# Masks of attention scores on 64-row halves, two groups of scores joined, one sum for the tokens' bound, and a new order, on one core of a Trainium2 chip

## The chip, the cores and the metric

The program runs on one core of a Trainium2 chip. The time is the device time of one execution in microseconds (us); several executions are timed and their median is given. The core has a matrix engine (PE), whose weight loads are shown apart (PEld), a vector engine (DVE), a scalar engine (ACT), GpSimd (POOL), and a queue engine (SP) that issues the transfers between the chip's main memory and the on-chip buffers.

## The reference, cut to what matters

Block-causal attention, whose result goes through two feed-forward layers. All arrays are 32-bit floats.

```python
B, H, S, D = 4, 8, 576, 64             # batch, heads, positions, head size
scores = q @ k.T / sqrt(D)             # a query of block i sees keys of blocks 0..i, blocks of 64
scores = where(block_i >= block_j, scores, -1e9)
attn = softmax(scores); x = attn @ v   # 2304 tokens of 512
h = x @ w_in;  x = (h * tanh(softplus(h))) @ w_out      # layer 0: 512 -> 2048 -> 512
h = relu(x @ w2_in);  out = (h * h) @ w2_out            # layer 1
```

## The kernel before

**Work and stages.** The 2304 tokens are cut into six chunks of 384 (`NX`). Chunks 0 and 1 hold the first 192 positions of the four sequences (`attention_lo`, products in 32-bit floats). Chunks 2 to 5 hold the other 384 positions of one sequence each (`attention_hi`, four pairs of heads in a chunk, 16 pairs in all). Each chunk then makes one pass through layer 0 and one through layer 1 (`PASSES`, twelve passes). Numbers there are split into two 16-bit halves, and each product is three 16-bit products (high by high, low by high, high by low). The last five passes of layer 0 and 1 that are listed in `SEVEN` use a scheme with fewer products (`first_seven`, `second_seven`).

**Scores.** `attention_hi` makes the scores of a pair of heads for three tiles of 128 queries (2, 3 and 4). The first head's 64 rows of queries and keys lie on partitions 0 to 63, the second's on 64 to 127, so a product of one head uses 64 rows of the array and the two heads' products go to two banks. `scores` issues six products (three for each head) and, where the tile reaches the end of what a query may see, two masks: a product of `above` (ones in the columns of the first 64 queries) with `never` (-1e24), which adds a huge negative number to the last 64 keys of those queries. The masks use all 128 rows. Tile 2 has 320 keys; beside it in the same banks the last 128 keys of tile 4 are scored; then tile 3 with 448 keys, then the first 448 keys of tile 4 without a mask. Each group is read by DVE (`peak`, the maximum, L919) and by ACT (`expo`, the exponential, L930), and the pair of banks, `ab`, is free for the next group only after that.

**The tokens' bound.** `chunk_scale` makes the scales of a chunk. Its `norm` bounds the length of a token: ACT squares two halves of the chunk (L1295, L1298), DVE adds them (L1301, L1302), PE sums over the partitions with a product of 384 columns (L1303), and DVE takes the maximum over the 384 tokens (L1305). It runs for 11 of the 12 chunk passes, five times in layer 0.

**Order.** Every piece of work is a task with an engine, some with a choice of engines. `PLAN` holds the whole order, one place and one engine for each task, and was worked out ahead by the planner in `Sched`, whose costs stand in the `sch.add` calls. Each engine takes its instructions in that order, and waits by semaphores for what they need. SP issues transfers in order too.

**Weights.** The split weights of the layers lie in main memory (`wspill`) and are loaded again in each pass, 512 KB at a time, into a ring of buffers (L1244); a load can start when PE has read the last of what the buffer held.

Of the kernel before, what the change touches and what calls it, by code (L numbers as in the profile page):

```python
# [68 lines left out]
def seg_len(tiles):  # L69
# [34 lines left out]
    "8=N{<R|WoF$|;}830D24i}Yj87=)Hj5tj)vNV0U79>g=xv+7ZqCI693uI$k_S@SP>L$>KQeN}qPK~~)-2XvUcDC@DfhxC*`^#k7bk=u#M5bXb3-;vEa4Xu01"
    "NO@cC;N744x;!Db$!qc#?^o(A@|g^i2W6{vm6iH`+EHq;>i^_-ZH0bA<VjhFmb>*0xmE_t*LYaKR#~oN2{!z$FG*urqF2du{PLjGmj(K*&e0k&Pshr$_)_&p"
    "{X(nDZ2e51kSg-2PSj8EcMF-OQ}I$O=`6eSeVwAeV$oP){iRk$?|1OVXSxC3=joI3u};%Zk@~vaqFv-sDT%h@!Rw1?nZmA#p!7PqpVQw$`rR^GM-!J)X08qZ"
    "x6S0Vj@4W7OA*sV8b}v;lNh}KGG9c)k$QvtM{5!Z=lL{kCwKBbPp>hp+50>ZY$@I31b)lbCh|1iI3k0HLq|D9lsd>Uy$9Uym9Bb9d+S|tjT~nGer&u=x1jIs"
    "AZ@qYqc>@3b5J|WGkANAY$39%$k*%f<yl>)KB#zH+RE?JLVuNCWsf%1zOqc)>3q3f+v;5Tl~a~zFYw=7C&^vXOt03p<m0E(hurTj^>sGcl1C)#;FX?IS1ZV9"
    "ayMHS@Tj5l!Cyu5zPvA$^uM6R*T-anbdWjvqKuOvvRq5)`|>X6nnF~*A*N&GTOwau-XxlHiQFie3;L?zjW=bQOyJ%)ouG$xq>L~h=nJySzADe7`8(kEDw!ys"
    ">(}}TxEW%;CUyh)>|y-^Ff>>u>T_UrARc}gWWI^)enfW+SH94<%m^a*g!CmRAD35noZ{Tq^dadb56cjwKM&4tmVc4$PsvUlr}u!C?b^`{lzv3vS=pqI>Wz4K"  # L110
    "ki5W(!SaZ_uMcS(tnMrQr6UNs0W9y<f9oThaxEBsLLSy7+JM(BWL{_OubWugRC?=A)Q|hMH+eN18F%Tww4Th+fqIADNuKng{#3*Jcasa(OTyeq)#(d{W)b%r"
    "sEpm@A$)W_UhE<d=vSb9iryr*lbtt7FK~Z@Ow#T$N*ii-Z7Vg2*Kq8qDz&MSRpnZwci?JUZBN#10ST9bk*l>iC@U%Lh|>japjV4~w3K@6YbGPfp@%@~mHMjI"
    "MB4@+zBc)G9}z7<#x$bp4k33NlC2G;kW|orv@-V!fWtb{pNxHyJ=LgZH-WFm$dU*35%l<*h(1UhTWJCxPY|`G$mfOR%mrH!nGN{+0ZdT^nHOzkUPns>B6?EK"
    "*>dDrS>jQU+FMG7Qnx*F?=W>dTld?dRI;J+v>ddnV4xE6x7};c!Yj{E@A}JQBCylrl0agANd+(cWTf%%`3T~we6~7*8kR@AcEBbtP@{Vz=REK31&!zJJ>>sj"
    "nPz)}z7u53VCu^WJI!o_Resl__7*hx(mo>($QtmFPL3X-rgr4rVQ`kF*W&X-I)fN&1T*PWt)F$hZN;t@WX~Mkr;ViuS+Pe~*xlq_CotKC+*xAllHYsq^$O6m"
    "Jg9?h@p)@-SXCBjYa-K;O57Ek^`vH8CzEwGC%5HlI~b}herY46jH{K4z{eC==L)#6Df@(oPlIviP^l(Th3b-z4MEqn;Hf<*`cAKrqDYvmL(%_o`AR<kCkgVd"
    "5qg)Sel*5o<zUe-^ku!A2#o`GuYt>I@-E0J%K0aBGu-`>ZX{Y2k#R&vP#>?L+SHTP#CAV;c@g$2DNCgb$as<6HDr-IO9iV!rQAgAtSG+Bm&@eIfLqhZ{qk`5"
    "K@e32H0Gky9<ZN6Zk*Q1@N`|Q@aZu&YjrvWpE|P0)`Eo`lh>0!kY9_M`X1Wl+U2?`?@jcoNOpDL>`czP4m=t#mkML1;L~H&)|Zjze3^!Ks}jkTREQP2Q>ROo"
    "ETxk<3g%1W*N3UGpXPydQ1Cf>HtAOF2RogIX~u(%he7aGF#NETkrq_0KFGWe3BAd}KahSe{ZT5<d7xyO?&aR^RFkftL5Ow^Y?c8#&gZmE@IyB_WwNOZ`?Rw;"
# [1768 lines left out]
```

## Time and profile before

| what | us |
|---|---|
| median of 3 runs | 872.76 (871.6 to 872.84) |
| the profiled execution | 872.93 |
| its span, first to last instruction | 871.2 |
| PE busy | 854.1 |
| DVE busy | 765.2 |
| ACT busy | 620.7 |
| POOL busy | 71.7 |

The profiled execution took 1.7 us more than its span, the time around the first and last instruction. Starts of matmuls are measured; their ends are modelled and overlap the next ones, so the cost of a matmul is read from one start to the next, not from its duration.

### The profile page before, as it was taken

How to read it: one execution, taken by the hardware profiler on the slowest of the kernel's cores; microseconds unless marked ns; L12 is line 12 of the kernel's file. 1: busy time of each engine (PE TensorE's matmuls, PEld its weight loads, DVE VectorE, ACT ScalarE, POOL GpSimd, SP SyncE). 2: the span in 40 equal slices, each digit the busy share in tenths (PEclk: the TensorE clock that was granted, in tenths of full speed). 3: DMA queues.
4: the chain of work that ended last, by engine and by line, in shares of the span. 5: the costliest groups of instructions: out<-in, count | busy, mean ns of one | idle time of the engine just before them, and what ended most of it. 6: DMA issues, size and time to landing. Idle time of an engine off the chain costs nothing.

```text
span 871.2 us, 19004 instructions
## 1 busy us (share of the span) xinstructions
PE 854.1 (98%) x7233; PEld 605.1 (69%) x7233; DVE 765.2 (88%) x1830; ACT 620.7 (71%) x1220; POOL 71.7 (8%) x78
## 2 busy tenths in 40 slices
PE   7999999999999999999999999999999999999997
PEld 6665455555555555555777677777878787799997
DVE  6999999999999998899999999996677777779876
ACT  6999999988898786887798987783334253266332
POOL 0000100112211000001000110001000001120100
PEclk9999999999999999999999999999999999999999
DMA  9995699998898998699999999996676746775572
GB/s 343 372 344 208 214 211 225 258 332 281 304 297 179 253 178 274 207 267 273 277 270 316 302 239 259 249 271 206 206 266 252 241 147 231 265 279 164 170 257 90
DMA packets 163930, 217.23 MB, mean 249 GB/s; under 512 B 107520, under 2 KB 125952, under 8 KB 163840
## 3 DMA queue, kind: packets, MB, share of 16 engines
q1 hardware_dynamic: 163840, 216.04, 82.9%
q8 instruction: 56, 0.92, 0.4%
q14 instruction: 34, 0.28, 0.1%
HBM read 160.95 MB, written 29.88 MB: 219 GB/s over the span
## 4 chain that ended last, share of the span: by engine, by line
PE 74%; DVE 10%; ACT 8%; DMA 5%; issue 2%; POOLq 0%; DVEq 0%; SPq 0%; ACTq 0%
PE acc L1453 27%; PE hp L1374 20%; PE hp L1341 12%; PE acc L1492 4%; DMA arena<-wspill 3%; PE bank L908 3%; PE bank L1016 2%; PE acc L1419 2%; DMA qk<-in_qk_dram 1%; ACT wsq L1160 1%; PE bank L1492 1%; ACT pad L930 1%; PE hp L1405 1%; DVE pb L817 1%; DMA arena<-in_w_dram 1%
## 5 line engine op out<-in xcount | busy, mean ns | idle before, releaser
L1453 PE MATMUL acc<-g,arena 128*128 128x384 f16 x1560 | 299.9, 326 | 1.2 <-DMA arena<-wspill 1.0
L1453 PEld LDWEIGHTS <-arena 128*128 128x128 f16 x1560 | 146.6, 98 | 82.6 <-issue 2.6
L1374 PEld LDWEIGHTS <-arena 128*128 128x128 f16 x1194 | 100.8, 98 | 14.4 <-DMA arena<-wspill 1.1
L1341 PE MATMUL hp<-xt,first 128*128 128x384 f16 x528 | 101.3, 326 | 0.8 <-ACT h L1346 0.7
L817 DVE SCALAR_TENSOR_TENSOR g<-h,cst,g 128x768 f16<-128x768 f32 x72 | 73.5, 1020 | 5.1 <-ACT g L1119 3.2
L1341 PEld LDWEIGHTS <-first 128*128 128x128 f16 x528 | 49.5, 98 | 40.4 <-issue 9.8
L1341 PE MATMUL hp<-xt,arena 128*128 128x384 f16 x384 | 75.1, 326 | 1.1 <-DMA arena<-wspill 0.9
L1374 PEld LDWEIGHTS <-first 128*128 128x128 f16 x816 | 69.2, 98 | 7.2 <-issue 0.3
L817 DVE SCALAR_TENSOR_TENSOR pb<-pad,st,pb 128x512 f16<-128x512 f32 (+2 forms) x96 | 71.5, 748 | 3.0 <-ACT pb L950 2.6
L930 ACT ACTIVATE pad<-bank,st,sq 128x448 f32<-128x448 f32 (+1 forms) x96 | 65.1, 681 | 8.8 <-DVE st L924 4.5
L1374 PE MATMUL hp<-arena 128*128 128x192 f16 x660 | 65.9, 246 | 0.0
L950 ACT ACTIVATE pb<-pad,st 128x384 f16<-128x384 f32 (+2 forms) x83 | 58.0, 713 | 4.9 <-DVE st L942 1.8
L919 DVE TENSOR_REDUCE st<-bank 128x1 f32<-128x448 f32 (+1 forms) x96 | 52.3, 572 | 6.9 <-PE bank L911 4.3
L1374 PE MATMUL hp<-xt,arena 128*128 128x192 f16 x534 | 54.4, 246 | 0.4 <-DMA arena<-wspill 0.4
L1346 ACT ACTIVATE h<-hp,cst 128x384 f32<-128x384 f32 x76 | 42.7, 575 | 16.6 <-PE hp L1341 15.9
L1341 PEld LDWEIGHTS <-arena 128*128 128x128 f16 x384 | 36.1, 98 | 26.0 <-DMA arena<-wspill 2.2
L1120 POOL TENSOR_SCALAR g<-h,cst 128x768 f16<-128x768 f32 x23 | 23.5, 1020 | 339.2 <-ACT h L1395 139.1
L1395 ACT ACTIVATE h<-h,cst 128x576 f32<-128x576 f32 x40 | 30.8, 771 | 28.8 <-DVE h L1393 28.7
L1391 ACT ACTIVATE h<-hp,cst 128x192 f32<-128x192 f32 x40 | 16.7, 418 | 47.5 <-PE hp L1374 40.8
L1374 PE MATMUL hp<-arena,first 128*128 128x192 f16 x480 | 50.2, 246 | 0.0
L1208 DVE TENSOR_TENSOR arena<-arena 128x256 f32<-128x256 f32 x96 | 41.5, 433 | 0.9
L1119 ACT ACTIVATE g<-h,cst 128x768 f16<-128x768 f32 x40 | 37.1, 928 | 6.2 <-PE acc L1453 2.9
(327 smaller groups left out, 1746.8 us busy)
## 6 DMA issues: line engine op xcount, KB each, us to landing
arena<-wspill SPq DMA_DIRECT2D x93, 512.0 KB, 4.7
arena<-in_w_dram SPq DMA_DIRECT2D x27, 1023.8 KB, 7.0
arena<-uspill SPq DMA_DIRECT2D x44, 512.0 KB, 5.6
wspill<-arena SPq DMA_DIRECT2D x24, 512.0 KB, 4.2
arena<-wspill SPq DMA_DIRECT2D x32, 384.0 KB, 4.2
qk<-in_qp_dram SPq DMA_DIRECT2D x16, 480.0 KB, 5.2
uspill<-xt SPq DMA_DIRECT2D x12, 512.0 KB, 5.0
uspill<-arena SPq DMA_DIRECT2D x12, 512.0 KB, 5.4
```

The source lines that it names most:

```text
L817: return sch.add("DVE", c_dve(n) + 62 * ap, lambda: nc.vector.scalar_tensor_tensor(dst(), a(), s() if ap else s, c(), op0, op1), r=r, w=w, ...
L919: t = sch.add("DVE", c_dve(o1 - o0), lambda hd=hd: nc.vector.reduce_max(st.t[:, 2 * j + hd:2 * j + hd + 1], pp.t[hd][:, o0:o1], axis=AX.X) ...
L930: t = sch.add("ACT", c_act(o1 - o0, True, 3), lambda hd=hd: nc.scalar.activation(pf[hd].t[r0:, k0:k0 + o1 - o0], view(hd)[r0:, o0:o1], AF. ...
L950: "ACT": ("ACT", c_act(n, False, 1), lambda pb=pb, pv=pv, s=s: nc.scalar.activation(pb.t[:, 0:i + 1, 0, :], pv(), AF.Copy, scale=s()), False),
L1119: "ACT": ("ACT", c_act(n, False, 1), lambda: nc.scalar.activation(dst(0), src(), AF.Copy, scale=s()), False),
L1208: plus(ENG["ts"], 256, lambda e, o=o, x=x, y=y, op=op: e.tensor_tensor(b(o), b(x), b(y), op), [], [q])
L1341: nc.tensor.matmul(out=hp.t[:, 0:n], lhsT=w.t[:, f % 2, a, 128 * k:128 * k + 128], rhs=x.t[:, c, k, 0:n], start=k == 0 and i == 0, stop=k ...
L1346: sch.add("ACT", c_act(n, True, 1), lambda f=f, o=o, hp=hp: nc.scalar.activation(h.t[:, o * n:o * n + n], hp.t[:, 0:n], (AF.Mish, AF.Relu) ...
L1374: nc.tensor.matmul(out=bank.t[:, o:o + z], lhsT=lhs, rhs=x.t[:, c, ks[k], :], start=start and k == 0 and i == 0, stop=k == 1 and i == 2, s ...
L1395: sch.add("ACT", c_act(3 * z, False, 1), lambda: nc.scalar.activation(h.t[:, z:2 * n], h.t[:, z:2 * n], fn, scale=hs()), r=[(cst, (HS, j)) ...
L1453: nc.tensor.matmul(out=acc.t[:, 0:n], lhsT=wo.t[:, f % 2, a, 128 * m:128 * m + 128], rhs=g.t[:, c, f % 2 * n:f % 2 * n + n], start=f == 0 ...
L1492: nc.tensor.matmul(out=acc[bank].t[:, o:o + c1 - c0], lhsT=lhs, rhs=g.t[:, c, z * b + c0:z * b + c1], start=j == 0 and (bank, o) in first ...
```

## The change

- The masks of `attention_hi` are cut in two: the first head's uses rows 0 to 63 of `above` and `never`, the second's rows 64 to 127. Each now sums 64 rows, not 128.
- The scores of tile 2 and of the last 128 keys of tile 4 become one task, so nothing stands between them on PE.
- In layer 0, `norm` no longer makes the maximum over tokens of their squared lengths: ACT sums the squares over all 384 tokens of a partition while it squares (`accum_out`), PE sums over the partitions with a product of 2 columns, DVE adds the two. The bound is then the sum over the chunk. Layer 1 keeps the old form (6 times).
- `never`, `signs` and the new sums `nf` lie in one small tile.
- Planning costs of one-column products (30 for 120 to 163), of the scores and of the products with the values are changed, and `PLAN` is another order.

```diff
+    small = cp.tile([128, 8], F32, name="small")
+    never, signs = small[:, 0:1].bitcast(BF16), small[:, 2:4]
+    R["nf"] = fixed([small[:, 4:6], small[:, 6:8]])
...
-        step = sch.add("PE", 150.0, lambda: nc.tensor.matmul(
+        step = sch.add("PE", 30.0, lambda: nc.tensor.matmul(
             out=vm.t[:, 0:1], lhsT=ones, rhs=upper(sv.t[:, 4:5]), start=True, stop=True), r=[(sv, 4)], w=[vm])
...
-        def scores(i, pp, o, k0, k1, mask=True):
-
-            a = tile_q(i)[0] - q0
+        def scores(pp, *spans):
 
             def mm():
-                for p, (u, w) in enumerate(((0, 0), (1, 0), (0, 1))):
-                    for hd in range(2):
+                for i, o, k0, k1, mask in spans:
+                    a = tile_q(i)[0] - q0
+                    for p, (u, w) in enumerate(((0, 0), (1, 0), (0, 1))):
+                        for hd in range(2):
+                            rows = slice(64 * hd, 64 * hd + 64)
+                            nc.tensor.matmul(out=pp.t[hd][:, o:o + k1 - k0], lhsT=qh.t[rows, u, a:a + 128], rhs=qh.t[rows, w, nq + k0:nq + k1],
+                                             start=p == 0, stop=p == 2 and not mask)
+                    for hd in range(2 if mask else 0):
                         rows = slice(64 * hd, 64 * hd + 64)
-                        nc.tensor.matmul(out=pp.t[hd][:, o:o + k1 - k0], lhsT=qh.t[rows, u, a:a + 128], rhs=qh.t[rows, w, nq + k0:nq + k1],
-                                         start=p == 0, stop=p == 2 and not mask)
-                for hd in range(2 if mask else 0):
-                    nc.tensor.matmul(out=pp.t[hd][:, o + k1 - k0 - 64:o + k1 - k0], lhsT=above, rhs=never[:, 0:1].to_broadcast([128, 64]), start=False, stop=True)
-
-            steps.append(sch.add("PE", 3 * (c_mm16(k1 - k0) + 16) + (110.0 if mask else 0.0), mm, r=[(qh, (p, j)) for p in range(2) for j in range(2)], w=[(pp, 0), (pp, 1)]))
+                        nc.tensor.matmul(out=pp.t[hd][:, o + k1 - k0 - 64:o + k1 - k0], lhsT=above[rows], rhs=never[rows, 0:1].to_broadcast([64, 64]), start=False, stop=True)
...
-            scores(i, pp, 0, 0, n)
+            scores(pp, (i, 0, 0, n, True), *([(4, n, 448, 576, True)] if i == 2 else []))
             if i == 2:
                 last, tail = R["st"].new(), R["tl"].new()
-                scores(4, pp, n, 448, 576)
                 steps.append(halves(vs, v3, sv, R["vm"].new()))
...
+            if l == 0:
+                nf, sq = R["nf"].new(), R["nsq"].new()
+                for i, k in enumerate(range(0, KC, 2)):
...
+                    sch.add("ACT", c_act(2 * n, False, 1 + seven), lambda i=i, src=src, s=s: nc.scalar.activation(
+                        sq.t, src(), AF.Square, scale=s, accum_out=nf.t[:, i:i + 1]), r=r, w=[sq, (nf, i)])
+                step = sch.add("PE", 30.0, lambda: nc.tensor.matmul(out=hp.t[:, 0:2], lhsT=ones, rhs=upper(nf.t), start=True, stop=True), r=[(nf, 0), (nf, 1)], w=[hp])
```

**Where the order moves, PE and one pair of heads.** On PE, at the scores of the fourth pair of heads (names: `q` the split queries and keys, `bank` the two banks of scores, `g` the activations of a pass, `acc` its results; L908 are scores, L911 masks, L1453 a pass). Before, the masks of tile 2 are followed by work of the pass, and the last keys of tile 4 come 24 rows later:

```order
L911 LDWEIGHTS above
L911 MATMUL bank_124<-never,above 128x64
L911 LDWEIGHTS above
L911 MATMUL bank_125<-never,above 128x64
L1453 LDWEIGHTS arena
L1453 MATMUL acc_3_1613<-g_1948,arena 128x384
```

Now (L909 are scores, L913 masks, both of 64 rows) the same two masks are followed at once by the last keys of tile 4:

```order
L913 LDWEIGHTS above
L913 MATMUL bank_125<-small,above 128x64
L913 LDWEIGHTS above
L913 MATMUL bank_126<-small,above 128x64
L909 LDWEIGHTS q_4_2058
L909 MATMUL bank_125<-q_4_2058 128x128
```

The second half of the group moved up to the first. In eight of the 16 pairs the two groups already stood side by side before.

**Where the order moves, PE at the start.** On PE, after the first two heads' products with the values (L1091 before, L1093 now). Before, the scores of a later head pair follow, then the turning of another's results (L1075):

```order
L1091 MATMUL acc_0_162<-pt,pb 128x64
L1052 MATMUL acc_1_263<-qk 128x192 x2
L1052 MATMUL acc_1_263<-qk 128x64
L1053 LDWEIGHTS above
L1053 MATMUL acc_1_263<-never,above 128x128
L1075 MATMUL acc_0_175<-ident,pt 128x128
```

Now a one-column product (L1165, it sums the squares of the first block of weights, which ACT makes in L1162) stands ahead of those scores, and a second head's scores ahead of the turning:

```order
L1093 MATMUL acc_0_164<-pt,pb 128x64
L1165 LDWEIGHTS onesq
L1165 MATMUL bank_126<-us_252,onesq 128x1
L1054 MATMUL acc_1_273<-qk 128x192 x2
L1054 MATMUL acc_1_273<-qk 128x64
L1055 LDWEIGHTS above
L1055 MATMUL acc_1_273<-small,above 128x128
L1054 MATMUL acc_1_286<-qk 128x192 x2
```

That one-column product stood 14 tasks further back before; everything on PE behind it now waits for ACT's squares too.

Elsewhere the order is shuffled by some ten places on PE and four on ACT. Some choices of engine move: of the high halves (L1119 to L1121) POOL made 44 and now makes 33, DVE 41 and now 52; of the copies (L790, L792) ACT made 110 and now 99, DVE 38 and now 49.

## Rows read from the trace of the kernel before

**Rows 1.** The page, busy time of each engine over the span.

```profile
PE 854.1 (98%) x7233; PEld 605.1 (69%) x7233; DVE 765.2 (88%) x1830; ACT 620.7 (71%) x1220; POOL 71.7 (8%) x78
```


**Rows 2.** Four stretches: start:end (us), length, busy us (instructions) by engine, PE clock, DMA, GB/s.

```profile
202.30:303.30 101.00, 100.83 (x704) 57.83 (x702) 95.05 (x241) 86.76 (x161) 15.96 (x15) 1.00 0.89 256
...
20.00:160.00 140.00, 136.97 (x811) 80.03 (x810) 135.05 (x357) 135.38 (x302) 8.65 (x11) 1.00 0.86 264
...
300.00:480.00 180.00, 178.47 (x1422) 112.78 (x1420) 166.42 (x382) 143.73 (x275) 5.56 (x5) 1.00 0.96 259
...
866.50:871.20 4.70, 0.00 (x0) 0.00 (x0) 1.70 (x4) 0.52 (x1) 0.00 (x0) 0.78 0.65 209
```

The engines of rows 2 are, in order, PE, PEld, DVE, ACT and POOL.

**Rows 3.** Waits of PE, longest sums first: us in all, times, longest.

```profile
PE acc L1052 <- DMA qk<-in_qk_dram: 4.5, 2, 4.2
PE acc L1075 <- DVE st L1067: 1.2, 1, 1.2
PE acc L1453 <- DMA arena<-wspill: 1.0, 3, 0.4
PE hp L1341 <- DMA arena<-wspill: 0.9, 1, 0.9
...
PE bank L1163 <- ACT wsq L1160: 0.6, 2, 0.4
```

**Rows 4.** The page, shares of the chain of work that ended last.

```profile
PE 74%; DVE 10%; ACT 8%; DMA 5%; issue 2%; POOLq 0%; DVEq 0%; SPq 0%; ACTq 0%
```

**Rows 5.** Timeline of PE near 303 us: start, duration, operation, matmuls in the row.

```profile
302.29 1.63 PE L1453 MATMUL acc<-g,arena 128*128 128x384 f16 x9
303.76 0.49 PE L1341 MATMUL hp<-xt,arena 128*128 128x384 f16 x2
```

**Rows 6.** Timeline of PE, 349.9 to 352.2 us, scores between two passes' products.

```profile
349.95 1.63 PE L1453 MATMUL acc<-g,arena 128*128 128x384 f16 x9
351.51 0.58 PE L908 MATMUL bank<-q 64*128 64x320 f16 x6
352.02 0.23 PE L911 MATMUL bank<-never,above 128*128 128x64 bf16 x2
352.09 0.16 PE L836 MATMUL bank<-sv,ones 128*128 128x1 bf16 x1
352.12 0.32 PE L1453 MATMUL acc<-g,arena 128*128 128x384 f16 x1
```

**Rows 7.** Timeline of PE, 334.5 to 336 us, two groups side by side.

```profile
334.58 0.58 PE L908 MATMUL bank<-q 64*128 64x320 f16 x6
335.09 0.23 PE L911 MATMUL bank<-never,above 128*128 128x64 bf16 x2
335.26 0.34 PE L908 MATMUL bank<-q 64*128 64x128 f16 x6
335.53 0.23 PE L911 MATMUL bank<-never,above 128*128 128x64 bf16 x2
335.61 0.65 PE L1453 MATMUL acc<-g,arena 128*128 128x384 f16 x3
```

**Rows 8.** Groups of DVE in `norm`, ACT's sum reads: busy us, mean ns, idle before.

```profile
L1301 DVE TENSOR_TENSOR nsq<-nsq,wsq 128x768 bf16<-128x768 bf16 x11 | 6.9, 625 | 0.7 <-ACT nsq L1298 0.6 <-ACT wsq L1295 0.2
L1305 DVE TENSOR_REDUCE cst<-hp 128x1 f32<-128x384 f32 x11 | 6.1, 555 | 3.3 <-PE hp L1303 3.2
L1302 DVE TENSOR_TENSOR nsq<-nsq 128x384 bf16<-128x384 bf16 x11 | 3.9, 352 | 0.0
...
L930 ACT ACTIVATION_READ_ACCUMULATOR pad<-bank,st,sq 128x1 f32 x96 | 18.8, 195 | 0.0
```

**Rows 9.** Group of the masks' weight loads: busy us, mean ns, idle before them.

```profile
L911 PEld LDWEIGHTS <-above 128*128 128x128 bf16 x96 | 5.5, 97 | 11.8 <-issue 10.1
```

**Rows 10.** The page, DMA issues of the weights: count, KB each, median us to landing.

```profile
arena<-wspill SPq DMA_DIRECT2D x93, 512.0 KB, 4.7
```

**Rows 11.** Timeline of PE at the start of the program, first matmuls.

```profile
15.91 1.06 PE L1052 MATMUL acc<-qk 128*128 128x192 f32 x6 [0.35 <-DMA qk<-in_qk_dram]
```

More of the change, by code (lines that the diff above doesn't have):

```diff
@@ L104 @@
[L104 to L119, printed above, removed]
@@ L168 @@
-    "*^TEz+?PVX@x-SDe%y{%6Yy;czW58TS~9&fyVKFa?e4&i^8x;A)7d%X?TL^#1Z~>!cMB^WhO+1=rmN#rA6*jYpFv0FzODNP<n1Sxudr_dcU|;7`uGIVZ^}La"
-    "=?X#`1i!1ebKNv%+;0$cI>pE%cfLbxVXn0W4JSFL5SCpH`dz*{L|A-LhUncOK3H;DQvw7QXVnc<@uKME{twD7w9lmf*~y)wAnSf{(Q}n|177m+esL;Bp1S|7"
-    "Qi1cz2mIqs^YLH-toNx~32{DmR%{9ShCJ?+V(&(FT~znKV>&T=oWr;GQlSe3Xmr1<mZNS95)J#E%`2(r>w}zGhs@(3)lfNBlQ*fXJV0-E5gDh^=@b?2Z_aWV"
-    "n8gVN(WnH`NuW)Epq2^R9$`fuyWMZZhtaMV7FVK|akXd%_Uz@khpM!je6B*Z*a_w<!Z(-U<two@6AYCNs(c~rNkj6jawy=b`g}6@*Zq&8Qk;>2ywm_&1=;6n"
@@ new lines @@
+    "58u?{Qx|zaenI1Eaxr<>Le8gV=Tn{9%XgeLi)c?k=QG){9u{mxmYgH4<qPy(NyY9Cc50B5lhJsxj-_T*qDB^=?YC6lue2e49H|{_H#wWUtcSNhqu!own^QZ_"
+    "Al`X;AB;6Z*OII6>%aOEIu6r|=o%Uj`)qdAk!Oi<8FUj6w-sx9V&zb3r4s+=K*n1AT`CfRhIlpyPp<&CkAZ=c$+Wuc{EseVZF_Xv&igj7XvnX>i2GP@b4<UH"
+    "Hppm56)r=@ucDeC&`rmC>w82wm-^61-jzD!rotn0i0BsBvk3m~j`W)Nye7UWP1YZz+H|I(??r<Pq_RAX?SrtP5KrWj?`5cxkD%!W?Aed4v$SbYoebHfGw4<f"
+    "`53^a4S2oXYyKhLIS6OXhw<0Iyz_WpK;F**5!>*6iX9f)en+SIuuQ37D@>n>2YSG%ztBCbq#mtO$ELsO74%dWakY>~9yMSSJXc5s8Vhpr@a=jkZ)x=0Ps9uL"
@@ L193 @@
+    "!yx>Bj=x`a"
 )
@@ L770, in tile_attention_moe @@
     nc.vector.memset(above[:, 64:128], 0.0)
-    never = cp.tile([128, 2], BF16, name="never")
     nc.vector.memset(never, -1e24)
-    signs = cp.tile([128, 2], F32, name="signs")
     nc.vector.memset(signs[:, 0:1], 0.25 * 0.125)
@@ L881, in scale_of @@
         def scale_of(pp):
-            steps.append(sch.add("PE", 150.0, lambda: nc.tensor.matmul(out=pp.t[:, 0:2], lhsT=ones, rhs=upper(sq.t[:, 8:10]), start=True, stop=True),
+            steps.append(sch.add("PE", 30.0, lambda: nc.tensor.matmul(out=pp.t[:, 0:2], lhsT=ones, rhs=upper(sq.t[:, 8:10]), start=True, stop=True),
                                  r=[(sq, 8), (sq, 9)], w=[pp]))
@@ L977, in attention_hi @@
         pp, pf = R["ab"].new(), [R["pf", 4].new() for _ in range(2)]
-        scores(4, pp, 0, 0, 448, False)
+        scores(pp, (4, 0, 0, 448, False))
         peak(last, 0, pp, 0, 448)
@@ L998, in mm_av @@
                 products(streams)
-            step = sch.add("PE", sum(3 * c_pair(nq - max(q0, 128 * c) + q0) for c in range(nch)) + 98, mm_av, r=[v3, *pts], w=[av])
+            step = sch.add("PE", sum(3 * c_pair(nq - max(q0, 128 * c) + q0) for c in range(nch)) - 41, mm_av, r=[v3, *pts], w=[av])
             step.rows = 0.86
@@ L1091, in mm_av @@
                 nc.tensor.matmul(out=av.t[:, 128:192], lhsT=vs.t[:, 128:256], rhs=pt.t[:, 0:64], start=False, stop=True)
-            step = sch.add("PE", c_f32(192) + c_f32(64) + 200, mm_av, r=[pt, vs], w=[av])
+            step = sch.add("PE", c_f32(192) + c_f32(64) + 300, mm_av, r=[pt, vs], w=[av])
             step.rows = 0.8
@@ L1162, in weigh @@
         sch.group = "norms", l, k, j0
-        step = sch.add("PE", 163.0, lambda: nc.tensor.matmul(out=sc.t[:, 0:size], lhsT=onesq, rhs=upper(us.t[:, NGRP:NGRP + size]), start=True, stop=True),
+        step = sch.add("PE", 30.0, lambda: nc.tensor.matmul(out=sc.t[:, 0:size], lhsT=onesq, rhs=upper(us.t[:, NGRP:NGRP + size]), start=True, stop=True),
                        r=[(us, ("sum", i)) for i in range(size)], w=[sc])
@@ L1265, in chunk_scale @@
         c = lambda a, k=1: cst.t[:, a:a + k]
-        step = sch.add("PE", 120.0, lambda: nc.tensor.matmul(out=sc.t[:, 0:m], lhsT=ones, rhs=upper(xm.t[:, 0:m]), start=True, stop=True), r=[xm], w=[sc])
+        step = sch.add("PE", 30.0, lambda: nc.tensor.matmul(out=sc.t[:, 0:m], lhsT=ones, rhs=upper(xm.t[:, 0:m]), start=True, stop=True), r=[xm], w=[sc])
         order.append((at, step))
```

176 lines of the change are left out of this document (98 added, 78 removed).

## Prediction

> **What bounds the kernel now.** I read the page's busy times first. PE is busy 98% of the span, DVE 88%, ACT 71%, POOL 8% [rows 1]. A busy PE is not yet the bound, since its rows are modelled, so I read the waits next. All of PE's idle time that was waited for is 11.5 us in eleven kinds, and the first transfer of the program is 4.5 us of it; no other kind exceeds 1.2 us [rows 3]. The chain that ended last runs through PE for 74% and through DVE and ACT for 18% [rows 4]. Then I read four stretches. From 202 to 303 us and from 300 to 480 us PE works without a gap while DVE and ACT have some room (95.0 and 86.8 us of 101; 166.4 and 143.7 of 180). From 20 to 160 us there is no room: PE has 137.0, DVE 135.1 and ACT 135.4 of 140 us. In all three the granted clock is 1.00, the upper of its two levels (2.4 GHz). After the last product 4.7 us remain in which PE does nothing, and the change doesn't reach them [rows 2]. So time taken from PE should come off the end, unless another engine or a transfer then ends last; in 20 to 160 us that is least sure.
>
> What a product costs is read from start to start. Nine products of 384 columns begin at 302.29 and the next begins at 303.76: 1.47/9 = 0.163 us each [rows 5], although each row shows a longer duration.
>
> **The price of a group of scores.** Look at what stands around the scores in [rows 6]. Nine products of 384 columns start at 349.95 and should end their share at 349.95 + 1.47 = 351.42. The scores start at 351.51, so 0.09 us went into the turn from products on 128 rows to products on 64. The scores are three pairs of 320 columns. The two heads of a pair run beside each other, since six products take 351.51 to 352.02, or 0.51 us, where one after the other they would need 6 x 320/384 x 0.163 = 0.81. Side by side they need 3 x 0.136 = 0.41, and the 0.10 left over is the turn back to 128 rows. A turn is thus about 0.10 us each way. Two masks on 128 rows take 352.02 to 352.09, 0.07 us, and a product of one column 352.09 to 352.12, 0.03 us.
>
> In [rows 7] the two groups stand side by side: scores of 320 columns 0.51 us (with a turn), masks 0.17 (0.07 and a turn), scores of 128 columns 0.27 (0.17 and a turn, so 0.057 a pair), masks 0.08. From 334.58 to 335.61 that is 1.03 us, and the turn into it makes 1.13.
>
> **The change, part by part.**
>
> *Masks on halves and the joined group.* With masks on 64 rows nothing turns between the parts: turn in 0.10, scores 0.41, masks m, scores 0.17, masks m, turn out 0.10, or 0.78 + 2m against 1.13. In tile 3 only the masks change (0.07 to m), and the last group of a head pair has none. A pair of heads has eight turns before (two for each of tile 2, the tail, tile 3 and the last group) and six after. It saves two turns and three old masks, less three new ones: 0.20 + 0.21 - 3m = 0.41 - 3m, sixteen times. That eight of sixteen groups were already neighbours makes no difference, since the full-row masks turned PE twice there too.
>
> No row shows m, a pair of 64-column masks on 64 rows. Below it is bounded by the columns alone, 64/384 x 0.163 = 0.03 us; above by a pair of 128-column scores, 0.06 us [rows 7], which has the same shape and twice the columns. I take 0.038: one of the old masks takes 0.035 [rows 6], and two heads' should start together, as their scores do. The saving is 16 x (0.41 - 0.114) = 4.7 us (3.7 with m = 0.06, 5.1 with 0.03).
>
> *The sum for the tokens' bound.* Five products of 384 columns become products of two: 5 x (0.163 - 0.03) = 0.7 us off PE. On DVE five times 0.625 + 0.352 + 0.555 = 1.53 us go [rows 8], 7.7 us in all, and a reduce of two columns comes in. ACT reads ten sums more at about 0.195 us [rows 8], 2 us. DVE gains the eleven copies and eleven high halves that ACT and POOL give up; at about 0.35 us (the 384-wide L1302) to 0.625 us (the 768-wide L1301) each that is 8 to 14 us, so DVE's total rises by a few us of the 106 that it has idle [rows 1], and ACT's falls by about as much. I cost this at nothing, because PE's products cover it outside 20 to 160 us. Without that cover it would cost up to those 6 us.
>
> *The start.* The one-column product L1165 now stands ahead of scores on PE, and waits for ACT's squares. Two such waits were 0.6 us before, the longest 0.4 [rows 3]. The scores behind it had themselves waited 0.35 us for their keys at 15.91 [rows 11], so part of the new wait overlaps that one. I take 0.3 us more (0 to 1.2, the longest wait for a computation in rows 3). Behind L1165 queue the scores, and behind those DVE's maxima.
>
> *Weights.* Loads of 512 KB land 4.7 us after their issue [rows 10], and PE waited 1.9 us for them in the two larger kinds [rows 3]. I compared PE's work between the product that frees a buffer and the first one that reads it again. Eleven loads had under 5.0 us of it (least 4.2), and in the new order four or five do (least 4.4). I take 0.3 us less waiting; the bounds are all 1.9 us gone, or as much again.
>
> *Sum.* -4.7 - 0.7 + 0.3 - 0.3 = -5.4 us, on the profiled execution's 872.93 (span 871.2 and 1.7 around it), which lies 0.2 us from the median of 872.76. That gives 867.5 us. A mask's bounds and the start's give 866.8 to 869.4, and the weights' widen it to 865.2 to 871.6 if every bound fell together.
>
> **The rivals.** A measurement of this kernel can tell a change of about 0.2%, 1.75 us: faster is under 871.0, slower over 874.5.
>
> *The weight loads set the masks' pace.* Each mask loads `above` anew, and such a load takes 97 ns in the trace [rows 9]. If a mask pair took that long, m = 0.097, the saving is 16 x (0.41 - 0.29) = 1.9 us, and the time 872.93 - 1.9 - 0.7 = 870.3 us. Against it: the old masks, each with its own load, step by 0.035 us [rows 6], and the 128-column pairs step by 0.057 with a load for each product [rows 7], so loads of this length already hide. I give it 0.08.
> The Trainium skill speaks for this rival ("TensorE: Matmul & The Clock Gate", section "LDWEIGHTS (loading the stationary operand)"): a load takes its columns over 1.2 GHz, whatever the rows, so that halving the rows halves nothing. That is 107 ns for 128 columns, and with m = 0.107 the change would give 2.1 us, 870.8 us. The trace agrees on the load's duration (97 ns), not on its setting the pace.
>
> *New waits eat it.* Of the sixteen pairs four lie in 20 to 160 us, where DVE and ACT are as full as PE [rows 2]. If those engines set the pace there, 4 x 0.30 = 1.2 us of the saving is lost, and the time is 868.7, still in the forecast's range. For no change at all another 2.5 us of waits would have to come, such as weights late by as much again as now. For it: a shuffled order has new close calls. Against: all of PE's waits after the first transfer are 7 us in a run of 870 [rows 3]. Time 871.0 to 874.5, chance 0.12; between this and the forecast (869.5 to 871.0, half of the saving eaten) 0.07 beside the loads' 0.08.
>
> *Slower: ACT becomes the bound between 202 and 303 us.* ACT has 101 - 86.8 = 14.2 us idle there [rows 2]. Between the same products of the passes the new order gives ACT about 8.6 us more work, each instruction at the mean duration of its kind in the trace, mostly pulled forward from later. If ACT kept all its idle time, since it waits for PE's and DVE's results in order, PE would be late by 8.6 us there, and the time would be 867.5 + 8.6 = 876.1 us. It is slower than now from 7.0 us on, so four fifths of the extra work would have to fall on PE's path. Against it: in 20 to 160 us ACT was 97% busy, and PE lost only 3 us of 140 [rows 2]. Chance 0.05.
>
> *More than the sum.* If PE's waits for weights go altogether, and the start costs nothing, the time is 867.5 - 1.6 - 0.3 = 865.6 us; with some of the other waits gone too it is less. Chance 0.12.
>
> **How the numbers follow.** The forecast, 865.7 to 869.5 us, has 0.56, the larger gain 0.12, the two that leave a small gain 0.15, no change 0.12, slower 0.05. Faster by over 0.2% is 0.56 + 0.12 + 0.15 = 0.83, the same 0.12, slower 0.05. I predict 867.5 us. The range leaves out about 0.1 on each side: below, what lies beyond 864.2, which takes in all of the weights' waits and 1.4 us of the others; above, what lies beyond 871.8, which takes in the loads' case and the first part of no change.
>
> **What would show it.** In the profile of the changed kernel a joined group should take 0.78 + 2m, about 0.86 us from the product before it to the one after, with m the step at L913, about 0.04 us; one near 0.10 shows the loads' case. Product L1299 should step by 0.03 us. PE's waits should still sum to about 11 us, with a new one at L1165 under 1.2 us. PE's busy time should fall by about 5 us. ACT's idle time between 200 and 300 us should still be over 5 us; if it is near zero while PE waits for ACT, the slower case holds. The prediction is wrong if turns cost as much as before inside the joined group, or if PE's waits rise by more than 3 us.

## The result and the profile after

| | before | after |
|---|---|---|
| median, us (6 runs each) | 872.23 | 863.25 |
| ratio after/before, 95% interval | | 0.9899 [0.9885, 0.9912] |
| profiled execution, us | 872.93 | 863.41 |
| its span, us | 871.2 | 861.6 |

The change makes the kernel 9.0 us faster. Forecast were 5.4 us, and the range ended at 864.2 us: the sign was right, the size was not.

The page of the changed kernel, busy time by engine (against [rows 1]):

```profile
PE 845.8 (98%) x7233; PEld 606.5 (70%) x7233; DVE 759.8 (88%) x1836; ACT 614.9 (71%) x1224; POOL 63.2 (7%) x70
```

PE lost 8.3 us of busy time, and the span 9.6. A joined group of scores, on the timeline of PE (L909 scores, L913 masks; columns as in [rows 6]):

```profile
346.28 0.65 PE L1352 MATMUL hp<-xt,arena 128*128 128x384 f16 x3
346.86 0.58 PE L909 MATMUL bank<-q 64*128 64x320 f16 x6
347.28 0.19 PE L913 MATMUL bank<-small,above 64*128 64x64 bf16 x2
347.31 0.33 PE L909 MATMUL bank<-q 64*128 64x128 f16 x6
347.48 0.19 PE L913 MATMUL bank<-small,above 64*128 64x64 bf16 x2
347.60 1.64 PE L1464 MATMUL acc<-g,arena 128*128 128x384 f16 x9
```

Three products of 384 columns end their share at 346.28 + 3 x 0.163 = 346.77, and the next work starts at 347.60: the group takes 0.83 us, where it took 1.13 [rows 7]. A mask pair steps by 0.03 us (347.28 to 347.31), and no turn stands inside. That is the structure that was forecast, with m at its lower bound.

What PE waited for in the changed kernel (us, times, longest; against [rows 3]):

```profile
PE acc L1054 <- DMA qk<-in_qk_dram: 3.7, 1, 3.7
PE hp L1054 <- DMA vs<-in_qk_dram: 1.8, 1, 1.8
PE hp L1352 <- ACT h L1357: 1.8, 4, 0.9
PE acc L1464 <- DMA arena<-wspill: 0.7, 2, 0.4
PE bank L1018 <- ACT pad L933: 0.5, 1, 0.5
...
PE bank L1165 <- ACT wsq L1162: 0.3, 2, 0.2
```

Two waits of the kernel before that [rows 3] leave out:

```profile
PE bank L908 <- ACT pad L930: 0.7, 1, 0.7
PE hp L1374 <- DMA arena<-wspill: 0.4, 1, 0.4
```

The three kinds of waits for weights, 2.3 us in all, have become one, of 0.7 us. The whole list fell only from 11.5 us to 10.1. But the list hides part of each wait, since a matmul of 384 columns is shown 0.33 us long and steps by 0.163. So I also summed, over all starts of matmuls, the step less what the columns take (0.42 ns a column, at least 27 ns) and less 0.097 us at a turn (a column of 32-bit floats counts more). This is PE's lost time, with the start before its first product; the rest up to the last product's start is its own work:

```
PE's lost time up to    50    150    200    300    450    650    end us | own work
before                13.7   18.9   20.6   22.0   24.7   27.2   28.8   |  837.4
changed               14.2   18.4   19.8   21.2   22.8   23.8   24.6   |  831.6
E1 (new work, old     13.7   20.1   21.3   23.1   25.7   29.8   31.3   |  832.0
    order)
E4 (full-row masks,   13.6   17.0   17.9   19.2   20.7   22.7   23.5   |  835.9
    new order)
E9 (old, then new)    13.9   20.3   21.6   23.6   27.6   29.4   30.2   |  831.9
E10 (new, then old)   14.1   18.3   19.6   21.1   22.3   25.5   27.0   |  831.7
```

Between the kernels before and after, own work falls by 5.8 us and lost time by 4.2; after the last product 0.4 us come in (5.0 to 5.4 us), which gives the 9.6 of the spans. The split is good to about 1 us: the floor of 27 ns counts part of an old mask's step as lost. With other floors the totals of all rows move together by several us, while the difference between the two kernels stays between 3.7 and 4.4 us. The own work answers to the forecast's 5.4. The lost time was forecast to stay. It rose by 0.5 us up to 50 us, and fell by 2.4 us from there to 450 us and by 2.3 us after that.

### The profile page after: what moved, and what is told of

It reads as the page before. It is cut to its first block, busy times and chain, and to the rows that moved or that the text cites. A ratio compares the mean times of both kernels' runs of the same rounds, so it can differ in the third digit from the quotient of the medians.

```text
span 861.6 us, 19020 instructions
## 1 busy us (share of the span) xinstructions
PE 845.8 (98%) x7233; PEld 606.5 (70%) x7233; DVE 759.8 (88%) x1836; ACT 614.9 (71%) x1224; POOL 63.2 (7%) x70
## 4 chain that ended last, share of the span: by engine, by line
PE 73%; ACT 6%; DVE 5%; DMA 4%; issue 1%; SPq 0%; ACTq 0%; DVEq 0%
PE acc L1464 28%; PE hp L1385 23%; PE hp L1352 10%; PE acc L1503 5%; PE bank L1018 3%; PE bank L909 2%; PE bank L1503 2%; DMA wspill<-arena 1%; DMA arena<-wspill 1%; ACT pad L933 1%; DVE st L922 1%; DVE arena L818 1%; DMA pt<-pb 1%; ACT h L1357 1%; DVE pb L818 1%
## 5 line engine op out<-in xcount | busy, mean ns | idle before, releaser
L1464 PEld LDWEIGHTS <-arena 128*128 128x128 f16 x1560 | 147.1, 98 | 83.8 <-issue 3.4
L1385 PEld LDWEIGHTS <-arena 128*128 128x128 f16 x1194 | 101.1, 98 | 15.2 <-issue 1.5
L818 DVE SCALAR_TENSOR_TENSOR pb<-pad,st,pb 128x384 f16<-128x384 f32 (+2 forms) x96 | 71.6, 754 | 2.8 <-ACT pb L953 2.5
L1352 PEld LDWEIGHTS <-arena 128*128 128x128 f16 x384 | 36.2, 98 | 24.0 <-issue 0.8
L1121 ACT ACTIVATE g<-h,cst 128x768 f16<-128x768 f32 x37 | 34.4, 930 | 13.5 <-PE acc L1464 9.2
L1503 PEld LDWEIGHTS <-arena 128*128 128x128 f16 x504 | 37.5, 98 | 0.0
```

The lines of the kernel that those rows point to most:

```text
L818: return sch.add("DVE", c_dve(n) + 62 * ap, lambda: nc.vector.scalar_tensor_tensor(dst(), a(), s() if ap else s, c(), op0, op1), r=r, w=w, ...
L1121: "ACT": ("ACT", c_act(n, False, 1), lambda: nc.scalar.activation(dst(0), src(), AF.Copy, scale=s()), False),
L1352: nc.tensor.matmul(out=hp.t[:, 0:n], lhsT=w.t[:, f % 2, a, 128 * k:128 * k + 128], rhs=x.t[:, c, k, 0:n], start=k == 0 and i == 0, stop=k ...
L1385: nc.tensor.matmul(out=bank.t[:, o:o + z], lhsT=lhs, rhs=x.t[:, c, ks[k], :], start=start and k == 0 and i == 0, stop=k == 1 and i == 2, s ...
L1464: nc.tensor.matmul(out=acc.t[:, 0:n], lhsT=wo.t[:, f % 2, a, 128 * m:128 * m + 128], rhs=g.t[:, c, f % 2 * n:f % 2 * n + n], start=f == 0 ...
L1503: nc.tensor.matmul(out=acc[bank].t[:, o:o + c1 - c0], lhsT=lhs, rhs=g.t[:, c, z * b + c0:z * b + c1], start=j == 0 and (bank, o) in first ...
```

## The experiments

All ratios are to the kernel before, run beside it on the same chip; 0.0010 is 0.87 us. A difference between two of them is good to about 1 us at best, and to 2 us for most pairs.

| run | work | order and engines | ratio, 95% interval |
|---|---|---|---|
| E1 | changed | before | 0.9968 [0.9958, 0.9979] |
| E2 | before | changed | 1.0036 [1.0021, 1.0052] |
| E3 | before, masks on 64 rows | before | 0.9976 [0.9966, 0.9986] |
| E4 | changed, full-row masks | changed | 0.9932 [0.9915, 0.9949] |
| E5 | changed, bound as before | changed | 1.0003 [0.9987, 1.0018] |
| E6 | before, half loads | before | 0.9978 [0.9968, 0.9987] |
| E7 | changed, half loads | before | 0.9939 [0.9925, 0.9953] |
| E8 | changed, half loads | changed | 0.9886 [0.9869, 0.9902] |
| E9 | changed | before, from 300 us changed | 0.9972 [0.9962, 0.9983] |
| E10 | changed | changed, from 300 us before | 0.9915 [0.9894, 0.9935] |
| E11 | changed | changed order, engines of before | 1.0388 [1.0368, 1.0408] |
| E12 | changed | order of before, changed engines | 1.0435 [1.0415, 1.0454] |
| E13 | changed, half maxima | before | 0.9936 [0.9919, 0.9953] |
| E14 | changed, half maxima | changed | 0.9858 [0.9839, 0.9878] |
| E15 | before, half maxima | before | 0.9975 [0.9962, 0.9988] |
| E16 | changed | changed, from 150 us before | 0.9993 [0.9979, 1.0006] |
| E17 | before, half loads and maxima | before | 0.9956 [0.9940, 0.9972] |
| E18 | changed, half loads and maxima | before | 0.9905 [0.9888, 0.9921] |

### Work or order: E1 to E5

E1 and E2 exchange the tables of the order, task by task:

```diff
-PLAN = (the order and engines of this kernel)
+PLAN = (every task at its place and on its engine in the other kernel)
```

E1: 

> All of the changed work (masks on halves, joined scores, the sum for the bound), but every task stands where it stood in the kernel before, on the engine it had there; a joined group stands at the first of its two. Theory A, the work gives what its terms say and the new order gives the rest: 872.2 - 5.2 = 867.0 us, with PE's waits for weights about as long as before (2 us or more in the list). Theory B, the work itself makes the other waits go (banks and engines come free earlier): about 863.5 us, with those waits shorter in the old order too. Between 865 and 866 both would have a part.

E2: 

> The work of the kernel before (full-row masks, two groups of scores, the maximum for the bound), in the order and on the engines of the changed kernel; the second of two groups stands right behind the first. Theory A: the order alone gives 872.2 - 3.8 = about 868.4 us, and PE's waits for weights fall to about 1 us. Theory B: the order alone gives nothing, 872 us, or is slower, since it was made for the other work.

E3 (the kernel before) and, the other way round, E4 (the changed kernel):

```diff
-lhsT=above, rhs=never[:, 0:1].to_broadcast([128, 64])
+lhsT=above[rows], rhs=never[rows, 0:1].to_broadcast([64, 64])
```

E3: 

> The kernel before, in its order, with the masks on 64 rows alone. By the prediction's terms: 48 mask pairs save 0.07 - 0.03 to 0.04 us each (1.6 to 1.9 us), and in the eight pairs of heads whose two groups are neighbours two turns of 0.10 us go (1.6 us): 3.2 to 3.5 us, or about 868.9 us. If the masks' weight loads set the pace (a pair at 0.097 us): 48 x 0.027 more and 1.6 less, about 871.9 us. If what is off is the turn, so that it costs more than 0.10 us, it is below 868.

E4: 

> The changed kernel in its own order, with the masks on all 128 rows again (the groups stay joined, but PE turns twice inside each). By the prediction's terms the loss is 16 x (0.20 + 3 x 0.07 - 3 x 0.03 to 0.04) = 4.7 to 5.1 us: 863.25 + 4.9 = about 868.1 us. If the masks were mis-sized and hold the gain that was not forecast, it is 870 us or more.

Neither theory's time came: E1 was slower than both had it, and with E2 theory A fell outright. The work alone gave 2.8 us in the old order, half of what it takes from PE, and the new order with the old work was 3.1 us slower than before. The lost time says why E1 gained so little: own work fell by 5.4 us, and 2.5 us of it came back as waits (31.3 against 28.8). PE's waits in E1:

```profile
PE acc L1054 <- DMA qk<-in_qk_dram: 3.9, 1, 3.9
PE acc L1464 <- DMA arena<-wspill: 2.9, 5, 0.8
PE hp L1352 <- ACT h L1357: 1.4, 3, 0.7
PE bank L909 <- ACT pad L933: 1.3, 2, 1.0
...
PE hp L1385 <- DMA arena<-wspill: 0.4, 1, 0.4
```

Waits for weights are 3.3 us, against 2.3 before, and those for the banks of scores 1.3, against 0.7.

E3 shows the same: by the starts, masks on halves take 3.7 us from the score groups (group lengths summed), and the time fell by 2.1. E4 against the changed kernel has 5.3 us more in its score groups and is 0.33%, 2.9 us, slower; PE's lost time is 1.1 us lower there. So no gain is hidden in the masks: in both orders the time falls by little more than half of what they take from PE. The joined groups and the sum add little in the old order: E1, which has them, is 0.08%, 0.7 us, faster than E3, which is not clear of noise.

The larger part lies in E4 against the kernel before: nearly the same work on PE (full-row masks, as many turns), yet 5.9 us faster, with 5.3 us less lost time. What it has is the new order and the sum for the bound. E5 takes the sum away again:

```diff
-            if l == 0:
+            if l == 9:
                 nf, sq = R["nf"].new(), R["nsq"].new()
...
-PLAN = (the order and engines of this kernel)
+PLAN = (the same, with the old bound's tasks put into it)
```

One more line, not shown, keeps the scale of layer 0 as it is.

E5: 

> The changed kernel in its order, halves and joined groups kept, but with the bound made the old way (maximum over tokens: DVE adds the squares, PE sums 384 columns, DVE takes the maximum). If the old work in the new order (E2) was slow because PE came to the bound's product before DVE had added the squares (5.6 us of waits there), this one loses the same 5.6 us and 0.7 of PE's work and is at about 869.5 us. If E2 was slow because of the masks and the split groups, this one is at 864 us.

E5 is as slow as the kernel before: 1.04%, 9.1 us, lost with the old bound, more than the 6.3 forecast for it. Here is the longest wait, in the changed kernel and in E5 (L1299 is the bound's new product, L1318 the old one, L1297 and L1310 ACT's squares, L1162 its squares of weights):

```profile
197.32 0.84 ACT L1297 ACTIVATE nsq<-xt 128x768 bf16<-128x768 f16 x1
...
200.67 0.74 PE L909 MATMUL bank<-q 64*128 64x448 f16 x6
201.25 0.19 PE L913 MATMUL bank<-small,above 64*128 64x64 bf16 x2
201.56 0.16 PE L1299 MATMUL hp<-small,ones 128*128 128x2 bf16 x1
202.03 0.65 PE L1352 MATMUL hp<-xt,first 128*128 128x384 f16 x3 [0.31 <-ACT h L1357]
```

```profile
200.58 1.05 ACT L1162 ACTIVATE wsq<-arena 128x1024 bf16<-128x1024 f32 x1
201.82 0.84 ACT L1310 ACTIVATE wsq<-xt 128x768 bf16<-128x768 f16 x1
...
200.54 0.19 PE L913 MATMUL bank<-small,above 64*128 64x64 bf16 x2
203.70 0.50 PE L1318 MATMUL hp<-nsq,ones 128*128 128x384 bf16 x1 [2.96 <-DVE nsq L1317]
203.99 1.17 PE L1352 MATMUL hp<-xt,first 128*128 128x384 f16 x3
204.95 1.17 PE L1464 MATMUL acc<-g,arena 128*128 128x384 f16 x3
205.91 1.01 PE L1352 MATMUL hp<-xt,first 128*128 128x384 f16 x3
```

With the sum, 0.31 us pass between the masks and the product. With the old bound PE stands for 2.96 us until DVE has added the squares. In the whole run there are four such waits:

```profile
PE hp L1318 <- DVE nsq L1317: 5.8, 4, 3.0
```

E2 has the same (5.6 us in five waits, the longest 2.5 us), and these waits are more than the 3.1 us by which it was slower. After the 2.96 us PE also steps by 0.32 us for 384 columns for a while (below).

But these waits show where E5's order has the old bound's tasks, not what the old bound must cost. Of the 2.96 us, 1.9 passed before ACT's second square was done at 202.66. The old form writes it to `wsq`, the one buffer that also holds the squares of weights, so it stands behind L1162. The new form writes both squares to `nsq`, and the second stands 4.5 us earlier, at 197.32. That is a part of the change which the section on it leaves out. In the other three waits the squares were done 5.0, 16.0 and 13.3 us before DVE's first add began, and DVE added them only right ahead of the product. The middle one of the three:

```profile
593.12 0.92 ACT L1313 ACTIVATE wsq<-xs,cst 128x768 bf16<-128x768 f32 x1
...
610.03 0.55 DVE L1316 TENSOR_TENSOR nsq<-nsq,wsq 128x768 bf16<-128x768 bf16 x1
610.61 0.36 DVE L1317 TENSOR_TENSOR nsq<-nsq 128x384 bf16<-128x384 bf16 x1
...
611.03 0.34 PE L1318 MATMUL hp<-nsq,ones 128*128 128x384 bf16 x1 [1.06 <-DVE nsq L1317]
```

In the changed kernel the new product starts 3.3 to 15.7 us after ACT's second sum, and the two adds take 0.9 us. The six bounds of layer 1 still have the old form in the same order, with the adds done 0.4 to 15 us ahead of the product, and PE waits at none of them. So E2 and E5 don't measure the order alone or the bound alone. The old bound with its adds further ahead, and with a buffer of its own for the second square, was not run, and what the sum is worth in the new order stays open between PE's 0.7 us and the 9.1.

### Which waits the old order has: E6 to E8, E13 to E15, E17, E18

Two reliefs, each in the old order with the old work, in the old order with the new, and one of them in the new. Half loads, from the seventh load of a ring on:

```diff
-pick = lambda t: ...[:, :, 0:768 if most else 1024]
+pick = lambda t: ...[:, :, 0:(768 if most else 1024) if w.idx < 6 else (384 if most else 512)]
```

E6: 

> The kernel before, but from its seventh load on in each ring a load of a pass's weights brings half of the bytes (the other half of the buffer keeps what it held, so the passes work on other numbers). Baseline for the next two. If waits for weights cost what PE's list shows, 872.5 - 2 = about 870.5 us; if the loads also held up other transfers, less.

E7: 

> E1 (the changed work in the old order) with the half loads of E6. Theory: in the old order the work that is taken from PE brings it sooner to weights that land no sooner, and half of the gain is given back there. Then with half loads the whole 5.2 us show against E6: about 865.3 us, 5 us under E1. Rival: the gain is lost at DVE and ACT; then this is 2.8 us under E6, about 867.7 us.

E8: 

> The changed kernel with the half loads of E6. If the new order's part of the gain is that PE waits less for weights, half loads have little left to take: 863.25 - 1 = about 862.3 us, and the distance to E7 shrinks from 7 us to 3 or less. If the new order gains elsewhere, the distance to E7 stays near 7 us: about 858 us.

The half loads gave 1.9 us to the kernel before, 2.5 to E1 and 1.1 to the changed kernel. So by these runs the new order gains only some 1.4 us of its 6.0 at the weights (the distance of E1 to the changed kernel, 0.69%; of E7 to E8, 0.53%), a difference that is not clear of noise. And the changed work was worth 3.4 us in E7 against E6, not 5.2: the theory that weights alone eat the rest fell.

Half maxima:

```diff
-nc.vector.reduce_max(st.t[...], pp.t[hd][:, o0:o1], axis=AX.X)
+nc.vector.reduce_max(st.t[...], pp.t[hd][:, o0:(o0 + o1) // 2], axis=AX.X)
```

E13: 

> E1 (the changed work in the old order) with DVE's maximum of the scores taken over the first half of a group's keys alone (96 reduces of some 0.57 us get about 0.2 us shorter or more; the softmax keeps its value, since any shift below overflow does). PE's and ACT's work and every place stay. If the old order loses the gain because DVE's results come late (for PE, and for the transposes that stand ahead of weights in SP's queue), 20 us less on DVE give most of it back: 866 us or less. If it loses it in the order of PE and of the loads themselves, it stays within 1.5 us of 870.5.

E14: 

> The changed kernel with the half maximum of E13, as its control. If the new order already hides DVE's lateness, little is left to gain: 262 to 863 us after the 863.3 of the changed kernel, that is 862 to 863. If DVE's lateness costs both orders the same, it falls as far as E13 does against E1.

E15: 

> The kernel before with the half maximum of E13. With it, E13 less this one gives what the changed work is worth in the old order when DVE is ahead: 5.2 us if DVE's lateness is what took half of it in E1, 2.8 us if not.

A lighter DVE gave 2.2 us to the kernel before, 2.8 to E1 and 3.6 to the changed kernel. So DVE's lateness costs every order, the new one no less, and it is not what sets the two orders apart. The work was worth 3.4 us (E13 against E15). Neither this nor the 3.4 us of E7 is clear of the 2.8 us without a relief. E14 is the fastest of all that compute the whole result; its shift holds only as long as no score in the second half of the keys lies so far above the first half's maximum that the exponential overflows.

E17: 

> The kernel before with the half loads of E6 and the half maximum of E13 together. Baseline for E18. If the two reliefs add, 872.5 - 2.1 - 2.2 = about 868.3 us.

E18: 

> E1 (the changed work in the old order) with both reliefs. With one of them the work was worth 3.2 us (E7 against E6) and 3.4 us (E13 against E15) in place of 2.8. If what eats the rest of the 5.2 us is the loads and DVE's lateness together, each stepping in where the other is taken away, this is 5.2 us under E17, about 863 us. If it is spread over more kinds of waits, some 3.5 us under E17, about 864.8 us.

With both reliefs the work is worth 0.51%, 4.4 us, where it was worth 2.8 without them, a rise just clear of noise. So weights and DVE's results together take some 1.6 of the 2.6 us that did not come through in the old order (5.4 less 2.8); the other 1 us stays unaccounted for, near what the intervals allow. That one relief alone lets the other cause step in is not shown: the two simply add, 2.5 + 2.8 us in E1 against 5.5 for both, and 1.9 + 2.2 in the kernel before against 3.8.

One such place could be followed in E1. The queue of SP, where L958 turns probabilities and L1246 loads weights:

```profile
386.88 3.78 SPq L958 DMA_TRANSPOSE late<-pb  x2
390.75 0.53 SPq L1246 DMA_DIRECT2D arena<-wspill  x1
391.33 0.42 SPq L1215 DMA_DIRECT2D uspill<-arena  x1
393.42 0.32 SPq L1246 DMA_DIRECT2D arena<-wspill  x1
```

The load at 390.75 stands directly behind two transposes, and had not PE to wait for any more. Three transfers of 512 KB then start within 2.7 us, the last of them lands after 6.4 us (the median of such loads in E1 is 4.9), and PE stands for it:

```profile
398.42 0.66 PE L1352 MATMUL hp<-xt,arena 128*128 128x384 f16 x3
399.88 0.50 PE L1464 MATMUL acc<-g,arena 128*128 128x384 f16 x2 [0.80 <-DMA arena<-wspill]
```

In E10, which has the same old order here, the same transposes and loads:

```profile
383.94 4.03 SPq L958 DMA_TRANSPOSE late<-pb  x2
388.06 0.53 SPq L1246 DMA_DIRECT2D arena<-wspill  x1
388.65 0.42 SPq L1215 DMA_DIRECT2D uspill<-arena  x1
391.22 0.32 SPq L1246 DMA_DIRECT2D arena<-wspill  x1
```

The transposes, whose start a result of DVE releases, are 2.94 us earlier, the last load, which waits for PE in both, only 2.2. So the two loads lie 3.2 us apart, the last lands after 5.4 us, and PE doesn't stand there. That the late transposes crowd the loads is read from the queue in these two runs; no run tested it.

### Where the new order gains: E9 to E12, E16

The changed work, with one table of the order up to some time and the other from there:

```diff
-PLAN = (one order)
+PLAN = (all tasks that one order starts by 300 us, in that order; the rest in the other order)
```

E9: 

> The changed work; the order and engines of the kernel before up to about 300 us, then those of the changed kernel. E1 (old order throughout) is at 870.5, the changed kernel at 863.3. By the waits in those two traces the new order saves some 2 us before 300 us and some 4.5 us after it (3.4 of weights, 1.2 of DVE's results). If those are what counts, this is at 870.5 - 4.5 = 866 us. If the gain is made early, 868.5 us. At the seam a transfer can be late, which neither says.

E10: 

> The mirror of E9: the changed work, the new order up to about 300 us, then the old one. If the gain is made after 300 us (weights and DVE's results in the last passes), 870.5 - 2 = 868.5 us; if early, 866 us. The two halves' gains should add up to the 7.2 us between E1 and the changed kernel.

E16: 

> E10 with the seam at about 150 us in place of 300: the changed work, new order and engines up to 150 us, the old ones after. E1 (seam at 0) was at 870.5, E10 at 864.9. If the gain of the early part is made while the scores and values of the first chunks fill DVE and ACT (20 to 160 us), this is at 865 to 866 us; if it is made between 150 and 300 us, at 869 to 870.5 us.

E10 keeps 4.6 of the 6.0 us and E9 nothing, which looks as if the new order won only by what it does in the first 300 us. The lost time says otherwise. E9 loses 4.0 us from 300 to 450 us, around its seam (E1 2.6, the changed kernel 1.6), but from 450 us on only 2.6, where E1 loses 5.6 and the changed kernel 1.8. So the new order gains late in the run too, and E9's seam hides it. And half of what E10 saves in lost time is collected behind its seam. At 300 us E10 is 2.0 us ahead of E1 (21.1 against 23.1); from there on, both in the old order, E10 loses 5.9 us and E1 8.2. The waits for weights in E10 are 1.3 us in its list:

```profile
PE hp L1385 <- DMA arena<-wspill: 1.1, 2, 0.7
...
PE hp L1352 <- DMA arena<-wspill: 0.2, 1, 0.2
```

against 3.3 in E1. E16 tells nothing of the stretch: behind its seam it loses 4.2 us between 150 and 200 us (17.5 to 21.7), some 3 us more than either order does there.

E11: 

> The changed kernel in its order, but every task that has a choice of engines on the engine that it had before (267 tasks differ). If the order of PE and of the transfers carries the gain, this stays within 2 us of 863.3; if the choice of engines carries it (DVE and ACT free at the right moment), it is at 868 us or more.

E12: 

> The mirror of E11: the changed work in the old order, with the engines of the changed kernel. If the engines carry the gain, it falls from E1's 870.5 to about 866 us; if the order carries it, it stays at 870 us or gets slower.

They were 34 and 38 us slower than before, far outside what either theory expected. The section on the change gives only the net shift of the choices, 11 copies and 11 high halves; 267 single tasks change their engine. Order and engines can't be told apart this way: a task on another engine stands there in a place that was made for other neighbours.

## Why the prediction was wrong, by its steps

- **The bound and what a product costs.** Right: PE's own work came straight off, 98% busy before and after.
- **Masks on halves and joined groups.** Right in mechanism, a little small in size. The price taken for a mask pair was 0.038 us, and it measured 0.03; summed over the lengths of all groups, 5.3 us left PE where 4.7 were forecast. How much of that reached the end is another matter: 2.1 of 3.7 us in E3. The rival in which the masks' loads set the pace needed 0.097 and is refuted by the timeline of the joined group. The rule of the Trainium skill that spoke for it ("TensorE: Matmul & The Clock Gate", section "LDWEIGHTS (loading the stationary operand)") holds for the load itself: with half the rows it still takes 94 ns (97 in [rows 9]). But the masks step by 0.03 us, so the loads lie under other products. The masks' loads now (least, median and longest in ns):

```profile
L913 PEld LDWEIGHTS <-above x96: 92/94/95, 82.9 to 545.7; 64*128 64x128 bf16 x96
```

- **The sum for the bound.** PE's part was right in size: three of the five new products step by about 0.03 us, and behind the other two PE waits for ACT's `h` (0.31 us at 202.03). The rest of the edit was costed "at nothing", on the ground that PE's products cover DVE's and ACT's work. DVE's total was to rise by a few us; it fell by 5.4. What the term left out is that the edit also frees the second square from the weights' buffer and shortens the chain from ACT's squares to PE's product. In the stretch shown, the product stands at 201.56, where it stood at 205.29 before. E5 loses 9.1 us with the old form, but mostly at waits that the places of its tasks decide, so by how much this term was wrong stays open.
- **The waits.** This is the step that failed: +0.3 us at the start and -0.3 for weights, with nothing for the other waits, so that the lost time would stay. It measured -4.2 us. At the start the size was near (+0.5 us up to 50 us), by luck: the first L1165 didn't wait at all, the waits for ACT's squares of weights fell from 0.6 to 0.3 us, and what came in was a longer wait for `vs` (0.5 to 1.8 us). At the weights the prediction had counted that eleven loads had little lead before and four or five in the new order, and still took 0.3 of 1.9 us; the list has 0.7 of 2.3 us left. The wait for a bank of scores (0.7 us) and the one for DVE's `st` (1.2 us, [rows 3]) went too, and those for ACT's `h` grew from 0.7 to 1.8 us. The list as a whole did what the prediction asked of it (10.1 us, "about 11"), since most of the 4.2 us lies in waits that it doesn't show.
- **Slower by ACT between 202 and 303 us.** Refuted. The stretch of the changed kernel (columns as in [rows 2]):

```profile
200.00:300.00 100.00, 99.35 (x708) 58.02 (x707) 93.36 (x232) 90.86 (x172) 13.35 (x14) 1.00 0.93 262
```

The same stretch of the kernel before:

```profile
200.00:300.00 100.00, 99.83 (x695) 57.16 (x694) 94.98 (x237) 87.76 (x159) 15.96 (x15) 1.00 0.89 258
```

ACT is busy 90.9 of 100 us, where it was 87.8: 3.1 us more in the same time, not 8.6, with 9.1 us idle, and PE is idle 0.65 us.
- **New waits eat it.** Not in the changed kernel, whose lost time fell. But it is what E1 shows of the same work in the old order: 2.5 us came back as lost time.
- **More than the sum.** This rival came true, at 9.0 us and not at its 7.3, and it had a chance of 0.12. By its mechanism, waits for weights gone and others with them, it is near what was seen: with the order of before the work brings 2.8 us, and the new order with the sum, but with full-row masks, brings 5.9 (E4), 5.3 of them lost time.

Not settled: why the new order loses so much less. The sum may have made part of it possible. It is no single wait that the lists show, loads and DVE's results both have a part in it by the reliefs, and the seams of E9 and E16 have costs of their own.

## What to carry to other kernels

Work taken from the bounding engine need not come through at its full price in a plan that was made for other work: where transfers and other engines finish just in time, here about half of it returned as waits (2.8 of 5.4 us came through). Forecast the order as a term of its own, then, and not as a shuffle that leaves the waits alone. When an edit shortens a chain between engines or frees a buffer, ask what can now stand earlier, not only what the removed instructions cost. And when an old form is put back into a new order to price it, look where its tasks stand: two adds placed right ahead of the product that needs them show their place, not their price. Count the short waits from starts to starts, since a list of idle times hides what lies under modelled ends.

## What was not expected of the hardware

Near the end of the 2.96 us in which PE stood in E5, its granted clock fell to 0.50, the lower of its two levels (1.2 GHz); PE's next products ran at it, and it came back to 1.00. The stretches of E5 (start:end and length, then PE with its instructions, and the other engines; the third number from the end is the clock):

```profile
201.00:203.50 2.50, 0.00 (x0) 0.00 (x0) 1.61 (x4) 2.41 (x4) 1.73 (x2) 0.94 0.97 339
203.50:206.60 3.10, 2.90 (x10) 1.38 (x11) 2.50 (x6) 2.30 (x4) 0.00 (x0) 0.50 0.78 297
206.60:212.00 5.40, 5.40 (x37) 3.29 (x36) 4.47 (x13) 3.31 (x8) 0.00 (x0) 1.00 0.58 201
```

A product of 384 columns stepped by 0.32 us there (three from 203.99 to 204.95), which adds some 1.4 us to a wait of 3, by the steps up to 206.76. The same followed the wait of 2.5 us in E2, from 207.6 us on. The wait of 1.8 us in E9 was followed by steps of the usual length. The single executions of E5 lie between 870.3 and 876.3 us with mean clocks from 0.995 to 1.000, a wider spread than that of the kernel before beside it (871.0 to 874.1, clocks of 0.999 and 1.000).
